# Sinkhorn attention with a max-of-two MoE layer: the zero matmuls, the GpSimd queue and the way W2 is turned

## The chip, the cores and the metric

The kernel runs on one core of one Trainium2 chip. The metric is the device time of one execution in microseconds (us), as the median of several executions. Engines are TensorE (PE; its weight loads are PEld), VectorE (DVE), ScalarE (ACT), GpSimd (POOL), SyncE (SP, which here only issues DMAs), and the 16 DMA engines.

## What is computed

Four batches, eight heads, 768 positions of 64 numbers. Each head's sequence is cut into 8 blocks of 96. Five Sinkhorn steps turn an 8x8 table per head into a soft permutation P, which mixes the blocks of k and v; each block of q attends to its mixed block. The heads are joined to 3072 tokens of 512 numbers, which go through a layer with two parallel weights and an elementwise maximum.

```python
for _ in range(5):
    P = np.exp(P - np.max(P, axis=-1, keepdims=True))
    P = P / (np.sum(P, axis=-1, keepdims=True) + 1e-09)
    P = P / (np.sum(P, axis=-2, keepdims=True) + 1e-09)
k_sorted = np.einsum('bhij,bhjcd->bhicd', P, k_b)
v_sorted = np.einsum('bhij,bhjcd->bhicd', P, v_b)
attn = softmax(scale * q_b @ k_sb.T)          # within each block
x = (attn @ v_sb)                             # -> 3072 x 512
out = np.maximum(x @ w1, x @ w2) @ w_out
```

## The kernel before

The order of instructions on each engine is that of the program text; nothing reorders it. Semaphore waits tie the engines together. Four PSUM buffers of 4 KB per partition serve all products in turn, so a product waits for the eviction of an earlier one. Inputs are loaded and cast to bf16 by DMAs on GpSimd's queue, in text order[...].

*Opening.* `keep_streaming` (L82) issues matmuls of zeros on TensorE: 86 of 142 columns at first, then six of 512 in each of Sinkhorn steps 4 and 5, each six waiting for a small memset on DVE (`late_zeros`). Meanwhile ACT and DVE make the Sinkhorn steps (L272 to L285), ending with p_bf. Between them DVE makes masks (`masks`), the batch 0 selections (`selections(0, nc.vector)`) and, later, two copies into maskJ (L824). GpSimd builds the identity `ident`, issues v0, k0 and q0 loads, then makes the selections of batches 1 to 3 and `one_j`, then issues all weight loads: W2 and W1 in columns, then W_out.

*Block diagonals and sorts.* `block_diagonals_first` (L367, L374) multiplies one_j and sel_v with p_bf, and DVE forms bd_k and bd_v. `sort_k` (three parts) and `sort_v` (four parts of 16 of the 64 columns) mix the blocks on TensorE; `turn_v` has laid v out by column first, on ACT and, for the last 16 of the 96 positions in a block, on DVE. Evictions go to ACT ("A") or DVE ("D") as the letter in the list says.

*Front.* The string `front` is the hand-written order of batch 0: k, v, tq (turn of q), SC (scores and exponential, eight units), VA (values, eight units), F (a request for zero matmuls in the next SC, VA or h unit), tx (turn of x), tw (turn of W2, two units of 16 transposes on TensorE), diff (W1 - W2), h (the hidden layer: two halves "a" and "b" per unit), pe (block diagonals of the other batches). Since max(h1, h2) = relu(h1 - h2) + h2, the kernel computes relu(x(W1 - W2)) W_out + x (W2 W_out). The first two quarters of W1 - W2 are made on GpSimd after the weight loads; the loads of k1, and later q1, v1, v2 and k2, follow them on GpSimd's queue.

*W2 W_out.* `w2_transposes` puts W2 with d_ff on the partitions into w2T, over PSUM; `w_product` (L668, four units) multiplies it with W_out.

*Passes.* Each batch then has numbered units on TensorE (the hidden layer, for batch 0 the four w_product in places 8 to 11, then twelve half output tiles), and a dictionary, `first_tail` for batch 0 and so on, says which steps of the next batch come after which unit: KS (key sorts), TQ, TURN (turn of v on DVE), SC, VS (value sorts), VA, TR (turn of x by DMA transpose on SP), pair_q (a copy of q on DVE), and `q_transposes` (DMA transposes on SP for batches 2 and 3).

Of the kernel before, what the change touches and what calls it, by code (L numbers as in the profile page):

```python
# [10 lines left out]
FP32 = mybir.dt.float32  # L11
# [5 lines left out]
def kernel(  # L17
# [16 lines left out]
    nc = tc.nc  # L34
# [34 lines left out]
    def ps_bf16(name):  # L69
        return psum.tile([128, 2048], BF16, tag="ps", name=name)  # L70
# [123 lines left out]
    load_k(0)  # L194
    load_q(0, True)

    sel_v, sel_k = {}, {}

    def selections(b, eng=nc.gpsimd):
# [12 lines left out]
            out=sel_k[b], in_=ident[0:G, b * 8 : b * 8 + 8].to_broadcast([G, 8, 16])  # L212
        )

    for b in range(1, B):
        selections(b)
    one_j = const.tile([G, 8 * 130], BF16, tag="one_j", name="one_j")
    nc.gpsimd.memset(one_j, 0.0)
    nc.gpsimd.tensor_copy(
        out=one_j.rearrange("g (j x) -> g j x", x=130)[:, :, 0:128].rearrange(  # L220
            "g j (h w) -> g j h w", w=16
        )[:, :, :, 0:2],
        in_=ident[0:G, 0:8].to_broadcast([G, 8, 2, NB]).transpose([0, 3, 1, 2]),
    )

    for t in range(2):
        load_w_columns(w2_sb, moe_w2, t, t + 1)
        load_w_columns(w1_sb, moe_w1, t, t + 1)
    load_w_columns(w2_sb, moe_w2, 2, 4)
    load_w_columns(w1_sb, moe_w1, 2, 4)  # L230
    load_w(wo_sb, moe_w_out)

    def w_difference(t, eng=None):
        n = DFF // 4
# [6 lines left out]
        if not eng:  # L241
            load["D"] += 600

    w_difference(0, nc.gpsimd)
    w_difference(1, nc.gpsimd)
    load_k(1)


    def turn_v(rows, eng, c0, c1):
# [39 lines left out]
            op=ALU.mult,  # L289
        )  # L290


    id64 = const.tile([128, 64], FP32, tag="id64", name="id64")
    maskJ = const.tile([128, 7, NB], FP32, tag="maskJ", name="maskJ")
    maskM = const.tile([128, 2, 8], FP32, tag="maskM", name="maskM")

    def masks(part):

# [161 lines left out]
    def sort_k(b, t, n=0, eng=None):  # L460
        kv = k_raw[b].rearrange("p (c d) -> p c d", d=D)
        ps = ps_f32("k_ps")
        keep_streaming(ps, n)

        for c in range(16):
            for par in range(2):
                m = (c + 8 * par) % 16
                r0 = par * 64
                nc.tensor.matmul(  # L469
                    ps[r0 : r0 + 64, m * 64 : (m + 1) * 64],  # L470
                    kv[r0 : r0 + 64, t * 16 + m, :],
                    bd_k[b][r0 : r0 + 64, :],
                    start=True,
                    stop=True,
                )
# [166 lines left out]
    w2T = big.tile([128, NFB, DMODEL], BF16, tag="w2T", name="w2T")  # L642
    wc = big.tile([128, HP, DMODEL], BF16, tag="wc", name="wc")

    def w2_transposes(t, eng):
        ps = ps_bf16("tw_ps")
        for n in range(16):
            fb, dmt = t * 4 + n // 4, n % 4
            nc.tensor.matmul(  # L649
                ps[:, n * 128 : (n + 1) * 128],  # L650
                w2_sb[:, dmt, fb * 128 : (fb + 1) * 128],
                ident,
                is_transpose=True,
                start=True,
                stop=True,
            )
        return lambda: evac(
            w2T[:, t * 4 : t * 4 + 4, :].rearrange("p f d -> p (f d)"),
            ps,
            2048,  # L660
            two_x=True,
            eng=eng,
        )

    def w_product(dmt):
# [119 lines left out]
    """.split()  # L785
    fills = [0]

    def fills_due():
# [3 lines left out]
    def front_step(step):  # L792

        eng = step[-1] if step[-1] in "AD" else None
        name = step[:-1] if eng else step
        kind = name.rstrip("0123456789ab")
        n = [int(x) for x in name if x.isdigit()]
        if kind == "F":
            fills[0] = 512
        elif kind == "k":  # L800
            sort_k(0, n[0], 1024 if step == front[0] else 0, eng)
        elif kind == "v":
            sort_v(0, n[0], 0, eng)
        elif kind == "tq":
            q_transposes(0, n[0], eng)
        elif kind == "SC":
            scores(0, n[0], fills_due())
        elif kind == "VA":
            values(0, n[0], fills_due())
        elif kind == "tx":  # L810
            x_transposes(0, n[0], eng)
        elif kind == "tw":
            w2_transposes(n[0], eng)()
        elif kind == "diff":
            w_difference(n[0])
        elif kind == "pe":
            block_diagonals([(0, 2), (0, 3), (1, 1), (1, 2), (1, 3)], 2)
        elif name[-1] == "a":
            moe_h_products(0, n[0], n[1], (0, 2), fills_due())
        else:  # L820
            moe_h(0, n[0], n[1], eng, (1, 3))

    for c, n, m in [(2, 2, 0), (4, 3, 1)]:
        nc.vector.tensor_copy(  # L824
            out=maskJ[:, c : c + n],
            in_=maskJ[:, m].to_broadcast([128, NB, n]).transpose([0, 2, 1]),
        )
    for step in front[:-26]:
        front_step(step)

    load_q(1)
# [14 lines left out]
    def sorts_and_scores(b):  # L846
# [27 lines left out]
    second_tail = {  # L874
        0: [lambda: q_transposes(2, 0), lambda: q_transposes(2, 1)],
        2: KS,
        4: SC[0:2],
        5: [VA[0]],
        6: SC[2:4],
        7: [VA[1], TR[0]],  # L880
        8: [VA[2], TURN[0]],
        9: [VA[3], TR[1], TURN[1]],
        10: SC[4:7],
        11: [VA[4], TURN[2]],
        12: [VA[5], TR[2], TURN[3], lambda: load_k(3), lambda: load_q(3)],
        13: [VA[6]],
        14: SC[7:8] + VS[0:2],
        15: [VA[7], TR[3]],
        16: VS[2:4],
        17: [lambda: pair_q(3, 0)],  # L890
        18: [lambda: pair_q(3, 1)],
    }
    SC, VA, TR, KS = sorts_and_scores(3)
# [69 lines left out]
```

## Time and profile before

| what | us |
|---|---|
| median of 9 executions | 167.37 (166.86 to 168.1) |
| the profiled execution | 168.1 |
| its span | 166.3 |
| TensorE busy | 160.5 |
| ACT, DVE, POOL busy | 83.1, 76.6, 32.2 |
| first exponential of batch 0 starts | 19.09 |
| first matmul of the hidden layer | 24.07 |
| GpSimd's first and second W1 - W2 start | 19.38, 22.17 |
| first w_product starts | 40.39 |
| first output product starts | 50.22 |

A line of the chain or the timeline gives start and duration in us, the engine, the line of the kernel or the tile, and how many instructions it merges. A line of the stage view gives, after the stretch, the busy time and the number of instructions of each engine. A line of the DMA view gives destination, source, the issuing queue, and the median time from issue to landing. SPq and POOLq are the issuing sides of SP and GpSimd. The page cuts the span into 40 slices of 4.16 us; a digit is a busy share in tenths. Matmuls are pipelined, so a mean duration of one (371 ns for 512 columns) is longer than the distance between two.

Loads through 62 us come in the order of GpSimd's queue: v0, k0, q0 (786 KB each in bf16), W1 and W2 (1.05 MB each), W_out (1.05 MB), k1, q1, v1 and v2, k2, q2, v3.

### The profile page before, as it was taken

How to read it: one execution, taken by the hardware profiler on the slowest of the kernel's cores; microseconds unless marked ns; L12 is line 12 of the kernel's file. 1: busy time of each engine (PE TensorE's matmuls, PEld its weight loads, DVE VectorE, ACT ScalarE, POOL GpSimd, SP SyncE). 2: the span in 40 equal slices, each digit the busy share in tenths (PEclk: the TensorE clock that was granted, in tenths of full speed). 3: DMA queues.
4: the chain of work that ended last, by engine and by line, in shares of the span. 5: the costliest groups of instructions: out<-in, count | busy, mean ns of one | idle time of the engine just before them, and what ended most of it. 6: DMA issues, size and time to landing. Idle time of an engine off the chain costs nothing.

```text
span 166.3 us, 4562 instructions
## 1 busy us (share of the span) xinstructions
PE 160.5 (96%) x2018; PEld 97.3 (58%) x2018; DVE 76.6 (46%) x173; ACT 83.1 (50%) x102; POOL 32.2 (19%) x55
## 2 busy tenths in 40 slices
PE   7999899999999999999899999999999999999992
PEld 7967778756554555557555544575655445654451
DVE  4859788556375564525258775070632420000011
ACT  3584994927239846055651344466456306652020
POOL 7997586150204000000004120000000000000000
PEclk9999999999999999999999999999999999999999
DMA  3999999999999996689602999989025284000333
GB/s 41 205 206 197 198 209 204 210 203 211 210 185 213 217 233 103 174 114 173 131 0 55 157 222 175 201 228 109 0 51 173 49 162 141 0 0 0 126 130 126
DMA packets 30404, 23.90 MB, mean 144 GB/s; under 512 B 16752, under 2 KB 25200, under 8 KB 30384
## 3 DMA queue, kind: packets, MB, share of 16 engines
q0 software_dynamic: 11040, 13.37, 48.2%
q1 hardware_dynamic: 19200, 10.17, 28.7%
q8 instruction: 16, 0.26, 0.6%
q10 hardware_dynamic: 144, 0.07, 0.1%
q14 instruction: 4, 0.03, 0.1%
HBM read 26.75 MB, written 6.29 MB: 199 GB/s over the span
## 4 chain that ended last, share of the span: by engine, by line
PE 85%; DVE 4%; DMA 4%; issue 2%; ACT 2%; ACTq 0%
PE out_ps L715 34%; PE h_ps L688 23%; PE fill_ps L82 7%; PE o_ps L586 4%; PE wc_ps L668 4%; DMA qT<-q_pair 4%; PE s_ps L559 4%; PE k_ps L469 2%; PE tq_ps L444 2%; ACT e L567 1%; DVE v_dc L257 1%; PE v_ps L534 1%; PE tw_ps L649 1%; PE v_ps L490 1%; PE tx_ps L624 1%
## 5 line engine op out<-in xcount | busy, mean ns | idle before, releaser
L715 PE MATMUL out_ps<-wo_sb,g 128*128 128x512 bf16 (+2 forms) x200 | 48.3, 371 | 0.1
L688 PE MATMUL h_ps<-xT,w_sb 128*128 128x384 bf16 x256 | 44.5, 326 | 0.0
L688 PEld LDWEIGHTS <-w_sb 128*128 128x128 bf16 x256 | 24.0, 98 | 15.6
L702 ACT ACTIVATE g<-h_ps 128x768 bf16<-128x768 f32 x27 | 21.8, 810 | 17.9 <-PE h_ps L688 17.8
L567 ACT ACTIVATE e<-s_ps 96x768 bf16<-96x768 f32 x32 | 23.8, 805 | 13.7 <-PE s_ps L559 13.5
L715 PEld LDWEIGHTS <-g 128*128 128x128 bf16 x200 | 17.1, 98 | 15.8
L715 PE MATMUL out_ps<-wc,xT 128*128 128x512 bf16 (+2 forms) x100 | 24.8, 370 | 0.0
L108 ACT COPY o<-out_ps 128x1024 f32<-128x1024 f32 x10 | 10.1, 1012 | 28.3 <-PE out_ps L715 25.6
L603 DVE TENSOR_TENSOR x<-o_ps,rs 96x512 bf16<-96x512 f32 x32 | 22.0, 687 | 1.1
L715 PEld LDWEIGHTS <-xT 128*128 128x128 bf16 x100 | 9.6, 97 | 11.2
L586 PEld LDWEIGHTS <-e 96*128 96x128 bf16 x256 | 11.8, 97 | 5.9 <-DVE v_sb L110 0.2
L597 DVE RECIPROCAL rs<-o_ps 96x8 f32<-96x8 f32 x32 | 6.4, 201 | 17.8 <-PE o_ps L586 17.7
L750 DVE COPY o<-out_ps 128x512 f32<-128x512 f32 (+1 forms) x2 | 1.2, 625 | 27.6 <-PE out_ps L715 27.6
L586 PE MATMUL o_ps<-v_sb,e 96*128 96x65 bf16 x256 | 12.9, 193 | 0.0
L108 ACT CAST v_sb<-v_ps 96x1024 bf16<-96x1024 f32 x10 | 9.8, 1015 | 2.5 <-PE v_ps L490 0.9
L110 DVE CAST kT<-k_ps 128x1024 bf16<-128x1024 f32 x7 | 8.3, 1215 | 5.8 <-PE k_ps L469 5.8
L704 DVE TENSOR_SCALAR g<-h_ps 128x768 bf16<-128x768 f32 x5 | 4.8, 956 | 12.3 <-PE h_ps L688 12.3
L559 PE MATMUL s_ps<-qT,kT 64*128 64x96 bf16 x256 | 8.6, 204 | 1.1 <-DMA qT<-q_pair 0.6
L559 PEld LDWEIGHTS <-kT 64*128 64x128 bf16 x256 | 6.1, 94 | 5.9 <-issue 3.1
L160 POOL DMA_DIRECT2D v_raw<-in_k_dram x3 | 2.4, 819 | 36.8 <-DVE rs L597 36.7
L82 PE MATMUL fill_ps<-fill 128*128 128x142 bf16 x86 | 8.3, 283 | 1.2 <-DVE fill L73 1.2
L110 DVE CAST v_sb<-v_ps 96x1024 bf16<-96x1024 f32 x6 | 7.3, 1216 | 4.5 <-PE v_ps L534 2.2
(96 smaller groups left out, 144.5 us busy)
## 6 DMA issues: line engine op xcount, KB each, us to landing
out_dram<-o SPq DMA_DIRECT2D x11, 512.0 KB, 3.3
v_raw<-in_v_dram POOLq DMA_DIRECT2D x8, 384.0 KB, 13.1
k_raw<-in_k_dram POOLq DMA_DIRECT2D x9, 256.0 KB, 10.0
w_sb<-in_moe_w_dram POOLq DMA_DIRECT2D x4, 256.0 KB, 8.3
w_sb<-in_moe_w_dram POOLq DMA_DIRECT2D x2, 512.0 KB, 11.0
wo_sb<-in_moe_w_out_dram POOLq DMA_DIRECT2D x2, 512.0 KB, 14.8
v_raw<-in_v_dram POOLq DMA_DIRECT2D x3, 256.0 KB, 4.9
q_raw<-in_q_dram POOLq DMA_DIRECT2D x4, 192.0 KB, 9.1
```

The costliest lines, as they stand in the source:

```text
L82: nc.tensor.matmul(ps[:, 0:w], w0, fill[:, 0:w], start=True, stop=True)
L108: nc.scalar.copy(out=out_ap, in_=in_ap)
L110: nc.vector.tensor_copy(out=out_ap, in_=in_ap)
L559: nc.tensor.matmul(ps[:, h2 * 512 + ii * 128 : h2 * 512 + ii * 128 + BLK], kT[b][rows, (hp * 8 + i) * BLK : (hp * 8 + i) * BLK + 128], rhs ...
L567: nc.scalar.activation(out=e[:, 0 : 8 * BLK].rearrange("p (t c r) -> p t c r", t=8, r=R), in_=ps[0:BLK] .rearrange("p (t f) -> p t f", t=8 ...
L586: nc.tensor.matmul(ps[:, h2 * 512 + ii * 65 : h2 * 512 + (ii + 1) * 65], e[:, (h2 * 4 + ii) * BLK : (h2 * 4 + ii) * BLK + 128], v_sb[:, m0 ...
L597: nc.vector.reciprocal(out=rs, in_=ov[:, :, :, 64])
L603: nc.vector.tensor_tensor(out=x, in0=ov[:, :, :, 0:D], in1=rs.to_broadcast([BLK, 2, 4, D]), op=ALU.mult,)
L668: nc.tensor.matmul(ps[:, 0:512], w2T[:, fb, dmt * 128 : (dmt + 1) * 128], wo_sb[:, fb, :], start=(fb == 0), stop=(fb == NFB - 1),)
L688: nc.tensor.matmul(h_ps[ch, t][:, m * 512 : m * 512 + TCH], w1_sb[:, hp, fb * 128 : (fb + 1) * 128], xT[:, b % 2, ch, hp % 2, hp // 2, :], ...
L702: nc.scalar.activation(out=g, in_=src, func=AF.Relu)
L715: nc.tensor.matmul(dst, g_tiles[b, ch, m // 2][:, m % 2, off : off + 128] if m < NFB else xT[:, b % 2, ch, hp % 2, hp // 2, off : off + 12 ...
```

## The change

- The first zero matmuls: 92 of 118 columns in place of 86 of 142. Those ahead of the first key sort: 640 columns in pieces of 320 in place of 1024 in pieces of 512. In `front` there is one more F, and two in a row now add up.
- GpSimd makes the selections of batch 0 and the two maskJ copies; DVE made them before. `one_j` is cleared as 32-bit words.
- GpSimd's queue is gated by three two-element copies into `seen`: the first reads p_bf, the second a piece of kT that the first key sort writes, the third the end of what the third transpose of W2 writes. The first W2 columns are issued after the first; the other weights after the second; the loads from q1 on after the third. Selections of batches 1 to 3 stand between the weight issues.
- W2 is turned by four DMA transposes on SP, one for each 128 columns of d_model, in place of 32 transposes on TensorE with two evictions. SP issues them ahead of every output store.
- `front` has a new order: the second key part first, scores of the second half of each sequence before the first half, later h units in another order.
- `first_tail` and `second_tail` have new places: key sorts and turns of q after w_product, value sorts at 17 to 19 in place of 12 to 14, values at 20 to 23 in place of 15 to 22, pair_q(2) in the second pass.

```diff
-    for b in range(1, B):
-        selections(b)
     one_j = const.tile([G, 8 * 130], BF16, tag="one_j", name="one_j")
-    nc.gpsimd.memset(one_j, 0.0)
+    nc.gpsimd.memset(one_j.bitcast(U32), 0)
...
+    selections(0)
-    for t in range(2):
-        load_w_columns(w2_sb, moe_w2, t, t + 1)
-        load_w_columns(w1_sb, moe_w1, t, t + 1)
-    load_w_columns(w2_sb, moe_w2, 2, 4)
-    load_w_columns(w1_sb, moe_w1, 2, 4)
-    load_w(wo_sb, moe_w_out)
...
-    w_difference(0, nc.gpsimd)
-    w_difference(1, nc.gpsimd)
-    load_k(1)
...
-        keep_streaming(ps, n)
+        keep_streaming(ps, n, most=320)
...
-    def w2_transposes(t, eng):
-        ps = ps_bf16("tw_ps")
-        for n in range(16):
-            fb, dmt = t * 4 + n // 4, n % 4
-            nc.tensor.matmul(
...
+    def w2_transposes(dmt):
+        nc.sync.dma_start_transpose(
+            out=w2T[:, :, dmt * 128 : (dmt + 1) * 128],
+            in_=w2_sb[:, dmt, :],
         )
...
-    keep_streaming(ps_f32("fill_ps"), 86 * 142, most=142)
+    keep_streaming(ps_f32("fill_ps"), 92 * 118, most=118)
...
-            selections(0, nc.vector)
...
+    for c, n, m in [(2, 2, 0), (4, 3, 1)]:
+        nc.gpsimd.tensor_copy(
+            out=maskJ[:, c : c + n],
+            in_=maskJ[:, m].to_broadcast([128, NB, n]).transpose([0, 2, 1]),
+        )
...
+    seen = const.tile([128, 3, 2], BF16, tag="seen", name="seen")
+    nc.gpsimd.tensor_copy(out=seen[0:G, 0], in_=p_bf[:, NB - 1, NB - 2 :])
+    load_w_columns(w2_sb, moe_w2, 0, 1)
+    selections(1)
+    selections(2)
...
     front = """
-        k0D k1A k2D v1D v2A v3A tq0D v0A tq1D SC1 SC0 F1
-        SC2 VA1 SC5 VA0 SC3 F2 VA2 SC4 F0 tx0D SC6 VA3
-        SC7 h00a VA4 tx1A tw0D h01a VA5 h01bA diff2 h00bA VA7 tx2A
-        tw1A h02a VA6 h02bA h11a diff3 tx3A h12a h03a h12bD h10a h10bA
-        pe2 h11bD h03bA h13a h13bA
+        k1A k0A v1D k2A v2A v0D tq0D v3A tq1D SC4 SC5 F2
+        F3 VA4 SC6 SC7 VA5 F0 SC0 VA6 SC1 VA7 F1 SC3
+        tx2D SC2 tx3D VA1 h10a VA0 VA2 h10bA h11a tx0A h11bA diff3
+        VA3 diff2 h13a h01a tx1D h03a h13bD h03bD h01bA h12a pe2 h00a
+        h02a h00bD h02bA h12bA
     """.split()
...
-            fills[0] = 512
+            fills[0] += 512
...
-            sort_k(0, n[0], 1024 if step == front[0] else 0, eng)
+            sort_k(0, n[0], 640 if step == front[0] else 0, eng)
...
-    for c, n, m in [(2, 2, 0), (4, 3, 1)]:
-        nc.vector.tensor_copy(
...
+    front_step(front[0])
+    c0 = int(front[0][1]) * 16
+    nc.gpsimd.tensor_copy(out=seen[:, 1], in_=kT[0][:, c0 : c0 + 2])
+    load_w_columns(w1_sb, moe_w1, 0, 1)
+    load_w_columns(w2_sb, moe_w2, 1, 2)
+    selections(3)
+    load_w_columns(w1_sb, moe_w1, 1, 2)
+    load_w_columns(w1_sb, moe_w1, 2, 4)
+    load_w_columns(w2_sb, moe_w2, 2, 4)
+    load_w(wo_sb, moe_w_out)
+    for dmt in range(HP):
+        w2_transposes(dmt)
+    w_difference(0, nc.gpsimd)
+    w_difference(1, nc.gpsimd)
+    load_k(1)
+    nc.gpsimd.tensor_copy(out=seen[:, 2], in_=w2T[:, NFB - 1, 382:384])
...
     first_tail = {
-        7: KS,
-        9: [TQ[0], TURN[0]],
-        10: [SC[0], TQ[1], TURN[1]],
-        11: SC[1:4] + TURN[2:4] + [lambda half=half: load_v(3, half=half) for half in range(2)],
-        12: VS[0:3],
-        13: VS[3:6],
-        14: VS[6:8] + [SC[4]],
-        15: [VA[0], lambda: pair_q(2, 0)],
-        16: [VA[1], lambda: pair_q(2, 1)],
-        17: SC[5:8] + [TR[0]],
-        18: [VA[2]],
-        19: [VA[3], TR[1]],
-        20: [VA[4]],
-        21: [VA[5], TR[2]],
-        22: [VA[6], VA[7], TR[3]],
+        11: KS,
+        12: [TQ[0]],
+        13: [SC[0], TQ[1]],
+        14: SC[1:4] + TURN[0:2],
+        15: SC[4:5] + TURN[2:4] + [lambda half=half: load_v(3, half=half) for half in range(2)],
+        16: SC[5:8],
+        17: VS[0:3],
+        18: VS[3:6],
+        19: VS[6:8],
+        20: [VA[0], VA[1]],
+        21: [VA[2], VA[3], TR[0], TR[1]],
+        22: [VA[4], VA[5], TR[2]],
+        23: [VA[6], VA[7], TR[3]],
     }
...
     second_tail = {
-        0: [lambda: q_transposes(2, 0), lambda: q_transposes(2, 1)],
+        0: [lambda: pair_q(2, 0), lambda: pair_q(2, 1)],
+        1: [lambda: q_transposes(2, 0), lambda: q_transposes(2, 1)],
         2: KS,
-        4: SC[0:2],
-        5: [VA[0]],
-        6: SC[2:4],
-        7: [VA[1], TR[0]],
-        8: [VA[2], TURN[0]],
-        9: [VA[3], TR[1], TURN[1]],
+        5: SC[0:2],
+        6: [VA[0], TURN[0]],
+        7: SC[2:4],
+        8: [VA[1], TR[0], TURN[1]],
+        9: [VA[2], TURN[2]],
         10: SC[4:7],
...
```

More of the change, by code (lines that the diff above doesn't have):

```diff
@@ L195 @@
     load_q(0, True)
+    id64 = const.tile([128, 64], FP32, tag="id64", name="id64")
+    maskJ = const.tile([128, 7, NB], FP32, tag="maskJ", name="maskJ")
+    maskM = const.tile([128, 2, 8], FP32, tag="maskM", name="maskM")
     sel_v, sel_k = {}, {}
@@ L290, in sinkhorn @@
         )
-    id64 = const.tile([128, 64], FP32, tag="id64", name="id64")
-    maskJ = const.tile([128, 7, NB], FP32, tag="maskJ", name="maskJ")
-    maskM = const.tile([128, 2, 8], FP32, tag="maskM", name="maskM")
     def masks(part):
@@ L643 @@
     wc = big.tile([128, HP, DMODEL], BF16, tag="wc", name="wc")
-    def w2_transposes(t, eng):
-        ps = ps_bf16("tw_ps")
-        for n in range(16):
-            fb, dmt = t * 4 + n // 4, n % 4
[L649 to L662, printed above, removed]
+    def w2_transposes(dmt):
+        nc.sync.dma_start_transpose(
+            out=w2T[:, :, dmt * 128 : (dmt + 1) * 128],
+            in_=w2_sb[:, dmt, :],
         )
@@ L811, in front_step @@
             x_transposes(0, n[0], eng)
-        elif kind == "tw":
-            w2_transposes(n[0], eng)()
         elif kind == "diff":
@@ L821, in front_step @@
             moe_h(0, n[0], n[1], eng, (1, 3))
-    for c, n, m in [(2, 2, 0), (4, 3, 1)]:
-        nc.vector.tensor_copy(
[L825 to L828, printed above, removed]
+    front_step(front[0])
[14 more added lines that the diff above has]
+    nc.gpsimd.tensor_copy(out=seen[:, 2], in_=w2T[:, NFB - 1, 382:384])
+    for step in front[1:-26]:
         front_step(step)
@@ L874 @@
     second_tail = {
-        0: [lambda: q_transposes(2, 0), lambda: q_transposes(2, 1)],
+        0: [lambda: pair_q(2, 0), lambda: pair_q(2, 1)],
+        1: [lambda: q_transposes(2, 0), lambda: q_transposes(2, 1)],
         2: KS,
-        4: SC[0:2],
-        5: [VA[0]],
-        6: SC[2:4],
-        7: [VA[1], TR[0]],
-        8: [VA[2], TURN[0]],
-        9: [VA[3], TR[1], TURN[1]],
+        5: SC[0:2],
[3 more added lines that the diff above has]
+        9: [VA[2], TURN[2]],
         10: SC[4:7],
-        11: [VA[4], TURN[2]],
-        12: [VA[5], TR[2], TURN[3], lambda: load_k(3), lambda: load_q(3)],
-        13: [VA[6]],
+        11: [VA[3], TR[1], TURN[3]],
+        12: [VA[4], lambda: load_k(3), lambda: load_q(3)],
+        13: [VA[5], TR[2]],
         14: SC[7:8] + VS[0:2],
-        15: [VA[7], TR[3]],
+        15: [VA[6]],
         16: VS[2:4],
-        17: [lambda: pair_q(3, 0)],
+        17: [VA[7], TR[3], lambda: pair_q(3, 0)],
         18: [lambda: pair_q(3, 1)],
```

## The prediction

> **What bounds the kernel now.** I read the engine shares of the page first, then the busy time by stage, then the chain of waits in order of time, and last the timeline of the stages that the change edits.
>
> ```profile
> PE 160.5 (96%) x2018; PEld 97.3 (58%) x2018; DVE 76.6 (46%) x173; ACT 83.1 (50%) x102; POOL 32.2 (19%) x55
> DMA  3999999999999996689602999989025284000333
> ```
>
> TensorE is busy for 160.5 of 166.3 us; nothing else passes half. But the DMA row is full in slices 2 to 15, up to about 62 us, so the first third has two limits: TensorE in program order, and loads that arrive just in time. The busy time by stage (TensorE, weight load, DVE, ACT, POOL, clock, DMA share, GB/s) gives the front:
>
> ```profile
> 12.04:18.70 6.66, 6.54 (x221) 5.53 (x221) 5.86 (x11) 4.00 (x5) 4.55 (x7) 1.00 1.39 201
> 18.70:24.14 5.44, 4.91 (x112) 3.51 (x109) 4.22 (x10) 5.24 (x8) 4.09 (x2) 1.00 1.31 202
> 24.14:38.83 14.69, 14.69 (x161) 10.08 (x163) 10.05 (x21) 8.80 (x11) 6.36 (x12) 1.00 1.23 208
> 38.83:52.32 13.49, 13.36 (x246) 7.66 (x247) 6.82 (x9) 7.36 (x11) 2.52 (x5) 1.00 1.13 200
> ```
>
> Sorts (DVE 5.86 of 6.66: evictions bound it), scores (ACT 5.24 of 5.44: exponentials bound it), then from 24.14 us on TensorE without a gap. The chain shows what stands in those stages:
>
> ```profile
> 1.20 10.90 PE fill_ps L82 x98
> 12.10 0.30 PE pe L367 x8
> ...
> 25.48 0.89 PE tw_ps L649 x16
> ...
> 29.19 0.89 PE tw_ps L649 x16
> ...
> 40.46 3.56 PE wc_ps L668 x16
> ```
>
> The zero matmuls at the start are themselves on the chain: the timeline has the last Sinkhorn step on DVE, which writes p_bf, from 11.06 to 11.27 us, yet the first matmul that reads it starts at 12.04. TensorE is 0.77 us late from filler. The two W2 turns cost 0.89 us each on a TensorE that is full.
>
> [...] the weight loads of L82, counted by the microsecond, double at about 7 us, though the page's clock column reads full throughout:
>
> ```profile
> 5.00:6.00 1.00, 1.00 (x9) 1.00 1.05 209
> 8.00:9.00 1.00, 1.00 (x18) 1.00 1.09 203
> ```
>
> [...] two qT transposes, 786 KB, were issued at 73.78 and had landed at 80.21[...], and beside loads they are slower still. [...]
>
> ```profile
> qT<-q_pair SPq DMA_TRANSPOSE x1, 6.4
> xT<-x SPq DMA_TRANSPOSE x1, 8.5
> ```
>
> The second was issued at 101.09 with q3 and an output store in flight (196 KB in 8.5 us to landing).
>
> **The change, part by part.**
>
> *Filler.* [...] So filler ends 0.57 us sooner, and the first product that reads p_bf starts at 11.47. p_bf itself comes at 11.19: the two sel_v copies that leave DVE stretched the fourth Sinkhorn step from 1.76 to 1.84 us. TensorE remains the later one: gain 0.57. On POOL the selections, one_j and mask copies end by about 9.8 (rows of 0.23 to 0.5 us after the last q issue at 7.97), well before use: nothing. The shorter fill ahead of the first key sort is hidden, since that sort waits for bd on DVE (12.70, then 12.91).
>
> *Sorts.* Now k1, k0, k2, v2, v3 leave by ACT at 1.01 us and v1, v0, tq0, tq1 by DVE at 1.2 and 0.96. Before, bd is ready at 12.70, the first k1 eviction starts on ACT at 14.15 (its products stood second, and ended at 14.05). After, bd is ready at 12.13, k1's 32 products (0.57) run first, and ACT starts at 12.97 and makes five evictions to 18.0. DVE ends the last turn of v at 13.3, evicts v1 from 14.15 to 15.37, v0 from 15.75 (its PSUM buffer is k0's, free at 15.0) to 16.97, tq0 to 17.93. The two mask copies (0.23) leave this row of DVE work. The first exponential starts near 18.45, not 19.09: 0.64, so the filler's gain and 0.07. The eight exponentials still pace the scores (5.97 us); one more fill of 512 columns stands under them and costs nothing. The last score ends at 23.50 instead of 24.14.
>
> *W2 turns.* 32 matmuls leave TensorE, 2 x 0.89 = 1.78 us, with evictions of 1.87 on ACT and 1.23 on DVE. After the last score the old order had 14.65 us of matmuls to 38.83; the new one has 8 x 1.30 of h, 4 x 0.24 of values, 3 x 0.34 of tx, 0.25 of pe (all durations from the chain): 12.65, so the front ends at 36.15. Two things could stop it there. GpSimd now issues the weights after p_bf and after the first key eviction (about 14.0), each 0.76: last wo issue near 20.4, differences at 2.12 each done by 22.5 and 24.6; h10 and h11 want them at 24.0 and 25.8. That fits. The DVE difference waits for the last W2 columns: 3.93 + 0.52 MB at 205 GB/s lie before their end at 25.3, plus 2 us to the semaphore (so the first difference, 17.5 by bytes, began at 19.38): 27.3 + 0.68 against a need at 27.65. I charge 0.3: front end 36.45, 2.4 earlier.
>
> *The transposes.* SP has nothing else queued then; the four need all of W2, so issue starts at 27.3. They move 1.05 MB beside 0.57 MB of W_out and 0.79 MB of k1 still due. With turns taken evenly at a total of 195 GB/s, three are through when 1.57 MB have moved, 8 us after 28.3, landed at 37.4; the fourth at 40. w_product reads one transpose each at 36.45, 38.3, 40.1 and 41.9. All four fit, with 2 us or less to spare.
>
> *The gate.* POOL's third seen copy holds q1, v1, v2, k2, q2 and v3 behind the third transpose. q1 is issued at 37.6 to 38.5 and lands by 44.5; its turn is wanted at 46.7 (w_product 7.3, keys 1.64, one output part 1.35). v1 and v2 land at 48.5 and 52.3; the value sorts want them, turned, at 57.5. k1 lands at 42.2 for 43.8. So later loads are hidden too.
>
> *The later order.* Scores spread over three units give back 0.4 of the 0.65 us that TensorE lost around 50 to 52.3 (exponentials on the chain). But the value sorts now stand just ahead of values: five evictions on ACT behind three exponentials, and v_sb complete about 0.3 us late. The x transposes of batch 1 are issued only at units 21 to 23 in place of 17 to 22: the second is issued some 1.9 us after its values (two reciprocals of 0.20, two products of 0.69) and lands 3.8 later, while TensorE reaches its readers in about 4.3 us: 1.1 lost. Against this the qT wait at 79 to 81 (0.6 + 0.1) goes, as scores start at unit 5, not 4. Together +0.3.
>
> Sum: -2.4 + 0.3 = **-2.1 us**. The profiled execution took 168.1 (span 166.3 and 1.8 around it), which would give 166.0; it was the slowest of nine. From the median, 167.37, I forecast **165.3**.
>
> **Unknown costs, from both sides.** Transposes of this shape: at best their plain bytes (5.2 us at 205 GB/s, no loss), at worst 8.5 us each as the row above: fourth landed after 60. I take even turns. POOL's timing beside DVE: nothing, or 1 us on the differences. The x wait: 0 to 2 us. [...]
>
> **Rivals.**
>
> A. *More is kept.* The x wait does not arise (landing 2.8 us, as some xT rows have) and the second pass loses less of its 0.82 us of TensorE idle (71.5 to 105.6, by stage): -2.4 - 0.3 - 0.7 = -3.4, 163.9. For it: the chain runs over DVE and DMA, not TensorE, at 73.8 to 80.2 and 91 to 97.7, so there is something to win. Against: ACT and DVE get less time between value sorts and values.
>
> B. *Gained in front, given back behind.* TensorE leads, and the same loads, later by the transposes' bytes, end the wait at the first turn of v or of q1: 1.05 MB at 195 GB/s is 5.4 us of transfer put into a row that is full to 62 us, of which 3 to 5 us of slack are eaten. A loss of 2 cancels: 167.4. For it: the DMA row. Against: q2 and v3 are now wanted a whole pass later.
>
> C. *Slower.* One mechanism: beside the loads the transposes get less than an even share, and w_product, in TensorE's order, waits with everything behind it. It decides when the fourth lands after 41.9, and the kernel gets slower once it lands after 44.0 (or the third after 42, by q1). At 4.8 us each, between the qT row alone and the worst xT row, the fourth lands at 28.3 + 19.2 = 47.5: 5.6 lost - 2.1 = +3.5, at 4.0 each +0.3; between them, at 4.4 each, +1.9: I put this case at 169.3. For it: the 8.5 row. Against: only 1.36 MB of loads compete, and they run dry by about 40.
>
> **How the numbers follow.** Forecast 0.46 (-1.0 to -2.9), A 0.18, B 0.12, C 0.24. Less than 0.5 us (0.3%) is what a measurement of this kernel can hardly tell from none; B lies mostly there (0.08), with 0.02 each way. Faster 0.46 + 0.18 + 0.02 = 0.66, same 0.08, slower 0.24 + 0.02 = 0.26. The range runs from 163.2 (A with its best costs) to 169.2, leaving the worse half of C out; the forecast's own is 164.5 to 166.4.
>
> **What would show it.** The one_j products near 11.5; first exponential near 18.5; last h_ps row of the front ending near 36.5 with no tw_ps; four DMA_TRANSPOSE rows on SP from about 27, landing by 40; no idle of L643 on w2T; q1's issue near 38; PE idle of about 1 us at the start of the second pass. I am wrong if TensorE stops ahead of wc_ps or tq_ps, if a chain through w2T appears, or if the front ends after 37.5.

## The result, and the profile after

The changed kernel takes 172.51 us (median of 10 runs, 170.65 to 173.57), the kernel before 167.4: a ratio of 1.027 with an interval from 1.024 to 1.030. It is slower by 4.5 us by the ratio and 5.1 by the medians, where 165.3 was forecast. The profiled execution took 170.92, with a span of 168.8 for 166.3. Of its twelve executions, with the profiled one, five took 170.7 to 171.7 at a granted clock of 0.998 or above, and seven 172.5 to 173.6 at 0.99; the profile shows one of the five.

The page's engine shares and its DMA row of the kernel after:

```profile
PE 158.3 (94%) x1993; PEld 93.5 (55%) x1993; DVE 75.6 (45%) x169; ACT 80.4 (48%) x100; POOL 33.5 (20%) x62
DMA  3999999997999999999704999984025253000333
```

TensorE has lost 2.2 us of work, and yet the span is 2.5 us longer: waits of 4.7 us are new. The DMA row, full up to slice 15 before (62 us), is now full up to slice 19 (80 us). The same four stages as shown of before (length; busy time of TensorE, weight load, DVE, ACT, POOL; clock, DMA share, GB/s):

```profile
12.04:18.70 6.66, 6.49 (x227) 5.49 (x220) 5.15 (x7) 5.61 (x7) 6.37 (x15) 1.00 1.39 198
18.70:24.14 5.44, 5.02 (x109) 3.62 (x109) 4.25 (x11) 5.30 (x8) 4.88 (x4) 1.00 1.28 186
24.14:38.83 14.69, 13.02 (x113) 7.96 (x112) 9.85 (x22) 4.73 (x7) 1.91 (x4) 1.00 1.23 200
38.83:52.32 13.49, 13.49 (x199) 7.32 (x198) 2.99 (x3) 5.07 (x7) 5.70 (x10) 1.00 1.01 179
```

The third row had TensorE busy throughout; now 1.67 us are idle in it. What ended those waits stands in the list of waits of the kernel after (who waited for what: us in total, times, longest):

```profile
POOL seen L821 <- DMA w2T<-w_sb: 13.8, 1, 13.8
PE h_ps L663 <- DMA xT<-x: 2.7, 1, 2.7
PE wc_ps L643 <- DMA w2T<-w_sb: 1.0, 1, 1.0
PE h_ps L663 <- DVE w_sb L231: 0.7, 1, 0.7
```

The chain of the kernel after puts them in order of time (start, length, what):

```profile
17.40 10.18 DMA w_sb<-in_moe_w_dram
...
27.67 10.37 DMA w2T<-w_sb
...
38.09 7.08 PE wc_ps L643 x32
...
53.96 1.50 ACT e L556 x2
55.45 0.90 ACT o L108
56.36 0.72 ACT e L556
...
64.46 1.22 DVE v_sb L110
...
69.76 5.25 DMA xT<-x
```

The opening is faster than forecast: the one_j product starts at 11.14 (12.04 before) and the first exponential at 18.13 (19.09). Up to w_product the gain holds in part. Behind it the chain leaves TensorE three times: for exponentials with an output eviction among them on ACT at 54 to 57 us, for v_sb at 64.5, and for a transfer of x at the start of the second pass. The first of these is no new loss: the chain before has exponentials at 50 to 52 us too, and TensorE is busy for 9.89 of the 10 us from 50 to 60, before 9.87. For v_sb TensorE waits 0.5 us, for x 2.7. That pass starts 3.06 us later than before (74.43 for 71.37), the third 2.33 later (107.76 for 105.43): 0.7 comes back in the second pass, and nothing after it.

### The profile page after: what moved, and what is told of

Read it like the earlier page. It is cut to its first block, busy times and chain, and to the rows that moved or that the text cites. A ratio compares the mean times of both kernels' runs of the same rounds, so it can differ in the third digit from the quotient of the medians.

```text
span 168.8 us, 4520 instructions
## 1 busy us (share of the span) xinstructions
PE 158.3 (94%) x1993; PEld 93.5 (55%) x1993; DVE 75.6 (45%) x169; ACT 80.4 (48%) x100; POOL 33.5 (20%) x62
## 4 chain that ended last, share of the span: by engine, by line
PE 69%; DMA 16%; DVE 5%; ACT 3%; POOL 2%; issue 1%; SPq 0%; ACTq 0%
PE out_ps L690 35%; PE h_ps L663 19%; DMA w2T<-w_sb 6%; DMA w_sb<-in_moe_w_dram 6%; PE wc_ps L643 4%; PE k_ps L458 3%; PE o_ps L575 3%; DMA xT<-x 3%; PE s_ps L548 3%; POOL w_sb L189 2%; ACT e L556 1%; PE v_ps L523 1%; PE tq_ps L433 1%; DMA p_sb<-in_sort_net_dram 1%; DVE colsum L276 1%
## 5 line engine op out<-in xcount | busy, mean ns | idle before, releaser
L108 ACT COPY o<-out_ps 128x1024 f32<-128x1024 f32 x9 | 9.1, 1013 | 28.3 <-PE out_ps L690 25.6
L575 PEld LDWEIGHTS <-e 96*128 96x128 bf16 x256 | 10.9, 98 | 6.4 <-DVE v_sb L110 1.0
L110 DVE CAST kT<-k_ps 128x1024 bf16<-128x1024 f32 x5 | 5.9, 1221 | 17.6 <-PE k_ps L458 17.6
L725 DVE COPY o<-out_ps 128x512 f32<-128x512 f32 (+1 forms) x2 | 1.2, 625 | 27.6 <-PE out_ps L690 27.6
L575 PE MATMUL o_ps<-v_sb,e 96*128 96x65 bf16 x256 | 12.3, 193 | 0.7 <-DVE v_sb L110 0.5
L110 DVE CAST v_sb<-v_ps 96x1024 bf16<-96x1024 f32 x7 | 8.5, 1219 | 5.6 <-PE v_ps L523 2.7
L108 ACT CAST v_sb<-v_ps 96x1024 bf16<-96x1024 f32 x9 | 8.9, 1007 | 2.2 <-PE v_ps L500 0.9
L643 PE MATMUL wc_ps<-wo_sb,w2T 128*128 128x512 bf16 x32 | 7.1, 379 | 1.0 <-DMA w2T<-w_sb 1.0
## 6 DMA issues: line engine op xcount, KB each, us to landing
wo_sb<-in_moe_w_out_dram POOLq DMA_DIRECT2D x2, 512.0 KB, 13.3
```

The costliest lines, as they stand in the source:

```text
L108: nc.scalar.copy(out=out_ap, in_=in_ap)
L110: nc.vector.tensor_copy(out=out_ap, in_=in_ap)
L575: nc.tensor.matmul(ps[:, h2 * 512 + ii * 65 : h2 * 512 + (ii + 1) * 65], e[:, (h2 * 4 + ii) * BLK : (h2 * 4 + ii) * BLK + 128], v_sb[:, m0 ...
L643: nc.tensor.matmul(ps[:, 0:512], w2T[:, fb, dmt * 128 : (dmt + 1) * 128], wo_sb[:, fb, :], start=(fb == 0), stop=(fb == NFB - 1),)
```

## The experiments

Four theories were open. **P**: the DMA engines take turns between SP's ring and GpSimd's by packets, not by bytes; transposes, in small packets, starve beside loads. **T**: the new order of the tails costs time by itself. **K**: the long waits let the granted clock fall, which makes the seven executions at 0.99. **R**, the rival of P: transposes of this kind are simply slow.

### Packets

The DMA view of the kernel after, by stretches of 2 us (packets, MB, share of 16 engines; q0 is GpSimd's ring, q1 is SP's), at 32 to 34 and then at 38 to 40:

```profile
q0 software_dynamic: 201, 0.36, 94.8%
q1 hardware_dynamic: 199, 0.05, 18.3%
...
q1 hardware_dynamic: 2113, 0.52, 124.2%
```

201 packets against 199, but 0.36 MB against 0.05. Alone, the transposes move ten times as much, 0.52 MB in 2 us or 260 GB/s. That already speaks against R. To see it without the gate and the new orders, the kernel before got nothing but the four DMA transposes in place of the two W2 turns:

```diff
-        SC7 h00a VA4 tx1A tw0D h01a VA5 h01bA diff2 h00bA VA7 tx2A
-        tw1A h02a VA6 h02bA h11a diff3 tx3A h12a h03a h12bD h10a h10bA
+        SC7 h00a VA4 tx1A h01a VA5 h01bA diff2 h00bA VA7 tx2A
+        h02a VA6 h02bA h11a diff3 tx3A h12a h03a h12bD h10a h10bA
...
+    for dmt in range(HP):
+        w2_transposes(dmt)
```

> The kernel before with the four DMA transposes of W2 alone, issued on SP as soon as W2 has landed, without a gate on GpSimd's queue, and without the two units on TensorE. Loads then run beside them until about 57 us. Theory P (packets in turn): some 4096 packets of 256 B against loads at 50 to 200 packets per us: the last transpose lands near 50 us or later, w_product (ready at 39) waits 8 us or more, with lost clock beside: 173 to 182. Rival R (10 us by themselves, whatever runs beside): they land by 40, nothing waits, 165.5 to 166.5.

Measured: 188.93 us (184.83 to 190.52). The loads, now without a gate, run beside the transposes to the end. The DMA view at 44 to 46 and at 52 to 54 us, then two of the waits of this kernel:

```profile
q0 software_dynamic: 64, 0.32, 86.2%
q1 hardware_dynamic: 63, 0.02, 7.0%
...
q0 software_dynamic: 129, 0.27, 99.9%
q1 hardware_dynamic: 131, 0.03, 17.5%
```
```profile
POOL w_sb L143 <- DMA w2T<-w_sb: 20.6, 1, 20.6
PE wc_ps L654 <- DMA w2T<-w_sb: 13.3, 2, 7.1
```

Packet for packet the rings are even, to within two; by bytes SP gets a ninth to a sixteenth of what GpSimd gets. How much depends on the loads' packets. At 39 to 41 us theirs are small, under 800 bytes (0.29 MB in 373), and SP gets a third:

```profile
q0 software_dynamic: 373, 0.29, 90.9%
q1 hardware_dynamic: 374, 0.10, 36.2%
```

P holds, and R falls. The size is larger than expected, and the clock has a part in it: its mean was 0.95 in all four executions, while TensorE waited 13.3 us for w2T. The gate in the changed kernel, which looked like a cost, is what keeps this from happening there.

### k1 behind the transposes

In the changed kernel k1 is the only later load ahead of the gate. Here it goes behind it.

```diff
-    load_k(1)
     nc.gpsimd.tensor_copy(out=seen[:, 2], in_=w2T[:, NFB - 1, 382:384])
+    load_k(1)
```

> The load of k1 is issued behind the third transpose of W2 in place of ahead of it, so that from about 31 us the transposes have the DMA engines to themselves. Theory P (each DMA engine takes packets in turn from the two rings, and a transpose packet of 256 B stands against a load packet of 1 to 2 KB): the first transpose lands near 34 us in place of 38.1, w_product no longer waits (it starts at 37.0), and the time falls by 1.0 to 1.5 us. Rival R (a transpose of this shape takes some 10 us by itself): it lands at 37 to 38 again, w_product waits as before, and the time stays at 172.5 or grows, as k1 comes later.

Measured: 171.05 (170.35 to 174.47), ratio 1.020 (1.015 to 1.026). SP's timeline has the four transposes issued in 7.8 us, not 11.4, and the third has landed at 35.8, not 39.9; w_product no longer waits for w2T. Its waits:

```profile
PE h_ps L663 <- DMA xT<-x: 2.9, 1, 2.9
PE tq_ps L433 <- DMA q_raw<-in_q_dram: 0.6, 1, 0.6
```

The first transpose took 6.3 us to landing, not 10.4, so the loads beside them decide how long they take, as P has it. But q1, now behind k1, comes late for its turn, and the x wait remains: the front's wait was the smaller part. The two runs at full clock, 170.35 and 170.39, are only some 0.4 us below those of the kernel after (170.65 to 171.67, median 170.81), so most of the 1.5 us between the medians (172.51 and 171.05) is the clock.

### The x wait

v3 is the load in GpSimd's ring when x is to be transposed. SP's timeline of the kernel after has three transposes issued over 5.71 us from 67.98, the first landed 6.3 us later; its DMA view at 68 to 70 us, and an issue of SP in the view at 64 to 66:

```profile
q0 software_dynamic: 66, 0.32, 77.3%
q1 hardware_dynamic: 68, 0.14, 19.9%
...
out_dram<-o SPq DMA_DIRECT2D x1, 512.0 KB, 8.9
```

SP's 68 packets carry 2 KB each (0.14 MB), where those of the W2 transposes carry 256 bytes (0.05 MB in 199). They belong to the output store that SP issued ahead of the transposes. The store takes turns with v3 and needs 8.9 us to landing, for a median of 3.3, and in the trace the packets of 256 bytes start only at about 71 us, when the store is nearly through. So v3 holds the x transposes up mostly through the store ahead of them.

A run held v3 behind the second x transpose, and another did that together with k1 behind the gate.

```diff
-        15: SC[4:5] + TURN[2:4] + [lambda half=half: load_v(3, half=half) for half in range(2)],
+        15: SC[4:5] + TURN[2:4],
...
-        21: [VA[2], VA[3], TR[0], TR[1]],
+        21: [VA[2], VA[3], TR[0], TR[1], after_x]
+        + [lambda half=half: load_v(3, half=half) for half in range(2)],
```

> The four loads of v3 are issued behind the second x transpose of batch 1 (a two-element copy that reads it) in place of some 15 us sooner. Theory P: the first x transpose lands near 71.5 in place of 74.4, TensorE's wait of 2.7 us at the start of the second pass falls below 0.8, and, as no long gap is left there, the runs at clock 0.99 become rare: 168.3 to 169.5 in all. Rival R: the x transposes take 5 to 6 us from issue as before, the wait stays, and the time is 172 to 173.

> Both moves of loads. Theory P: the two gains add, 167.2 to 168.3, no wait over 0.8 us on w2T or xT. Rival R: no less than 172.

Both missed: 184.19 (177.68 to 185.97) and 184.15 (179.42 to 186.1). The first x wait did go (0.5 us), but v3 now stands beside the fourth x transpose and those of qT. The chain of the run with v3 alone, its DMA view at 88 to 90 us, and its stretches ahead of and from 86 us:

```profile
74.09 20.47 DMA xT<-x
```
```profile
q0 software_dynamic: 71, 0.35, 97.8%
q1 hardware_dynamic: 69, 0.02, 8.4%
```
```profile
78.00:86.00 8.00, 2.29 (x46) 1.45 (x41) 1.95 (x2) 1.82 (x2) 0.00 (x0) 0.81 1.25 49
86.00:94.00 8.00, 0.00 (x0) 0.00 (x0) 0.00 (x0) 0.00 (x0) 0.00 (x0) 0.50 1.10 174
```

Where the x transpose issued ahead of it, with GpSimd's ring empty, landed in 2.9 us, the fourth took 20.5. The time was missed since I asked only which transposes v3 would leave, and not which it would meet. Turns by packets fit the second half of these 20.5 us, at 174 GB/s in all. In the first half both rings together moved only 49 GB/s; taking turns doesn't explain that, and its cause is open. The clock, at 0.50 from 83 us on, adds to the loss.

### The clock

Zero matmuls stand in the two waits, 11 of 512 columns ahead of the second pass and 4 ahead of w_product.

```diff
         ps = ps_f32("wc_ps")
+        keep_streaming(ps, 4 * 512 if dmt == 0 else 0)
...
-        units = [lambda ch=ch, t=t: moe_h(b, ch, t) for ch in range(2) for t in range(4)]
+        units = [
+            lambda ch=ch, t=t: moe_h(b, ch, t, n=11 * 512 if (b, ch, t) == (1, 0, 0) else 0)
+            for ch in range(2)
+            for t in range(4)
+        ]
```

> The changed kernel with 11 zero matmuls of 512 columns (2.4 us) ahead of the first hidden unit of the second pass and 4 (0.9 us) ahead of the first w_product, where TensorE waits 2.7 and 1.4 us for transposes. Theory K (the runs at mean clock 0.99 lose about 1.7 us because a gap on TensorE drops its clock to half for a few us): the gaps are filled, all runs are at clock 1.0, and the median is 170.5 to 171.2 in place of 172.5. Rival: the split of the changed kernel's runs into 170.7 and 172.6 has another cause; then the split stays and the median is 172 to 173.

Measured: 171.7 (171.04 to 172.01), ratio 1.025 (1.021 to 1.029). The time is a little above what was expected. In the profile, of the slowest of the four, the zeros are no longer than the waits that they replace (2.4 us for 2.7, 0.9 for 1.0), but the opening is 0.3 later, the wait for the W2 columns 0.4 longer, and TensorE waits 0.8 for q1. Still, all four runs had a clock of 1.00; none fell to 0.99, though four are few.

All runs together say more. In three kernels TensorE waits 2.7 to 2.9 us at one place (the kernel after, k1 behind the transposes, and v3 behind the qT transposes, below), and 12 of their 20 executions have a mean clock of 0.99 or less. In four kernels with the same opening and no such wait (this one and, below, W2 on TensorE, the old first tail, both old tails) none of 40 has. So K holds as far as this: such a wait makes a fall likely. It is not the only cause, since 3 of 19 executions of the kernel before, beside the last run below, have a clock of 0.99 or less too, and its longest wait behind the start is 0.6.

In the profiles the clock falls to half (0.50 in the row from 86 us above): for 17.1 us in the run with v3 behind x, and for 3.4 in that with v3 behind the qT transposes (a mean of 0.59 from 94 to 98 us). One fall of 3.4 us at half clock loses 1.7 us, about what lies between the two groups of the kernel after (medians of 172.7 and 170.8). Ahead of the fall TensorE was idle for 2.8 us in the latter, and in the last run below for no more than 0.5 at once behind the start. The falls of the kernel after itself are in no profile.

### W2 on TensorE again

The changed kernel with the two W2 turns back in its front (tw0A ahead of diff3, tw1A ahead of h01b), and without the gate:

```diff
+        elif kind == "tw":
+            w2_transposes(n[0], eng)()
...
-    for dmt in range(HP):
-        w2_transposes(dmt)
...
-    nc.gpsimd.tensor_copy(out=seen[:, 2], in_=w2T[:, NFB - 1, 382:384])
```

> The changed kernel with W2 turned on TensorE again (two units in its new front order, evicted by ACT) and without the gate on w2T, so that the loads from q1 on are issued some 15 us sooner. Theory P: no wait for w2T; the front ends 1 us later than in the changed kernel by 1.8 us of matmuls less its waits; v3 has landed before the x transposes, so the wait at the second pass is under 1.2 us, and the clock stays at 1.0: 167.3 to 169. Rival R2 (the new places in the tails cost the time by themselves, whatever the loads do): 170 to 172.

Measured: 169.25 (168.4 to 169.69), ratio 1.012 (1.009 to 1.016), just above what was expected. So W2 by DMA with its gate costs 3.3 us. But the median of the kernel after falls among its executions at lower clock. At full clock its five have a median of 170.81, and these four of 169.25: 1.6 us are waits and transfers, 1.7 the clock. Where the waits lie is seen at the start of the second pass, 72.09 for 74.43. This kernel's x wait, and the DMA view of it at 70 to 72 us:

```profile
PE h_ps L677 <- DMA xT<-x: 0.5, 1, 0.5
```
```profile
q1 hardware_dynamic: 991, 0.25, 66.1%
```

GpSimd's ring is empty there. The timelines of GpSimd (start, length) show why. Of the kernel after, and then of this one:

```profile
41.01 2.10 POOL L169 DMA_DIRECT2D v_raw<-in_v_dram  x4
...
57.85 1.56 POOL L169 DMA_DIRECT2D v_raw<-in_v_dram  x3 [3.09 <-DVE v_dc L250]
```
```profile
56.22 1.55 POOL L169 DMA_DIRECT2D v_raw<-in_v_dram  x3 [0.92 <-DVE v_dc L250]
```

With the gate, the last v loads are issued 1.6 us later into rings that still hold what the gate kept back, and end at about 72 us; without it they end by 68, and the store ahead of x takes 4.3 us to landing, not 8.9. First out_ps comes at 46.74 with the transposes and at 47.25 without: in front the change of W2 wins 0.5 us, as TensorE work less its waits, and at the second pass it is 2.3 behind. Of the 2.8 lost between, 2.7 are the x wait, through a load that nobody waited for; the kernel here has 0.5 of that wait still to come, behind its first two matmuls of the pass.

### The tails

On top of that, the first tail of the kernel before (without its two q pairings, which the new second tail does), and then both its tails:

```diff
     first_tail = {
-        11: KS,
-        12: [TQ[0]],
...
+        7: KS,
+        9: [TQ[0], TURN[0]],
...
```

> Base: e5_w2_on_pe (169.25 us). The first tail is that of the kernel before, the second that of the kernel after (pair_q at its unit 0). Theory F (the whole 1.7 us between e5 and e7_old_tails lie in the first tail: x transposes at its end, the split exponentials, v_sb): 167.0 to 167.8, x wait below 0.5. Rival S (part of it lies in the second tail): 168.2 to 169.2, with TensorE idle between 71 and 105 us above that of e7_old_tails.

> As the one before, and with the two tails of the kernel before: only the opening, the sorts, the front order, GpSimd's gates on p_bf and kT and the zero matmuls are those of the change. Theory P: the start of the scores 0.96 us sooner is kept to the end: 166.0 to 166.9. Rival R3 (the opening's gain is lost again in the front or at the loads): 167.2 to 168.5.

Measured: 167.22 (166.88 to 167.85), ratio 0.9995 (0.998 to 1.001), and 167.59 (167.36 to 168.43), ratio 1.0016 (1.000 to 1.003). The first hit, the second missed by 0.7 in favour of its rival. So the new first tail costs 2.0 us, and the new second tail wins some 0.4, with intervals that still overlap. (The kernel before took 167.38 beside the run with both old tails, and 167.35 beside the other.) The engines' busy time by stretches, with the new first tail (W2 on TensorE) and then with the old one:

```profile
60.00:71.00 11.00, 10.35 (x173) 5.92 (x167) 8.63 (x14) 4.84 (x5) 0.00 (x0) 1.00 0.80 200
71.00:75.00 4.00, 3.49 (x34) 2.10 (x33) 3.61 (x9) 1.75 (x2) 0.00 (x0) 1.00 0.66 143
```
```profile
60.00:71.00 11.00, 11.00 (x121) 6.05 (x120) 5.24 (x12) 3.22 (x4) 0.00 (x0) 1.00 0.87 175
71.00:75.00 4.00, 4.00 (x26) 2.32 (x24) 1.84 (x5) 2.45 (x3) 0.00 (x0) 1.00 0.86 78
```

Crowded into units 17 to 23, value sorts and values leave DVE 12.24 us of work in 15 (8.63 and 3.61); spread from unit 12 on it was 7.08 (5.24 and 1.84), and TensorE never stopped. TensorE's own idle time can't be read from the first of these traces: it holds 2006 of 2025 matmuls, and a missing one leaves a hole of up to 0.16 us. Of the 0.65 us that look idle from 60 to 71, such holes make more than half. The kernel after, whose trace is complete, waits 0.5 there for v_sb. That the crowding causes the 2.0 us fits these rows and the x wait of 0.5 us, which is gone with the old tail, but no run tests it alone; the two spans differ by 1.2 (166.6 and 165.4), and the rest is in no profile.

What of the opening's 0.9 us is left with the old tails? Nothing: w_product starts at 40.38, before at 40.39. The chain of the kernel with both old tails, and two waits of its TensorE:

```profile
17.49 10.45 DMA w_sb<-in_moe_w_dram
...
28.03 0.70 DVE w_sb L231
28.78 1.47 PE h_ps L677 x8
```
```profile
PE o_ps L575 <- ACT e L556: 0.4, 1, 0.4
PE h_ps L677 <- ACT w2T L108: 0.4, 1, 0.4
```

The new front wants the W2 columns as soon as the loads bring them: they are on the chain, and TensorE waited 0.3 for them in the run with the old first tail and 0.7 in the kernel after. Here the lead goes mostly to other things: 0.4 to the eviction of a W2 turn, whose place in this front I had chosen, 0.2 to one more fill of 512 columns, and some to waits in the scores, 0.4 and 0.2 where they were 0.3 and 0.2.

A last attempt at the x wait held v3 behind the qT transposes of batch 2, still with W2 on TensorE and the new tails, the turns of v3 two units later:

```diff
         1: [lambda: q_transposes(2, 0), lambda: q_transposes(2, 1), after_q]
+        + [lambda half=half: load_v(3, half=half) for half in range(2)],
```

> Base: e5_w2_on_pe (169.25 us; x wait of 2.8 us before the second pass). The two loads of v3 are held on GpSimd behind the last qT transpose of batch 2, and its four turns come two units later. Theory X (the 2.8 us wait for xT is there because the v3 loads stand beside the x transposes, and packets of the two rings alternate): the wait falls below 1.0 and the first h_ps of the second pass starts at 70.3 to 71.4 for 72.1; no transpose needs more than 8 us; time 167.0 to 168.3. Rival L (the x transposes are late because the order issues them late): the wait stays above 2 and the time at 168.9 to 169.8. If v3 then comes late for its turns, a wait on v_raw shows between 80 and 95 and takes the gain back.

Measured: 172.65 (171.15 to 173.3), ratio 1.031 (1.027 to 1.035). The base was misread: the 2.8 us that I named as its wait were the transfer's length on the chain, and TensorE waited 0.5, here too. So this run says nothing on X; it shows another price. v3 landed at 92.4, its turn stood on DVE waiting 3.4 us, the values' products queued behind it, and TensorE stopped for 2.8. The stretches after that:

```profile
90.00:94.00 4.00, 1.27 (x20) 0.56 (x18) 1.58 (x4) 1.50 (x2) 0.50 (x1) 0.98 1.13 176
94.00:98.00 4.00, 3.90 (x25) 1.80 (x26) 1.40 (x3) 0.81 (x1) 1.95 (x3) 0.59 0.75 111
```

After the stop TensorE is busy but at a mean clock of 0.59: part of the wait is paid a second time, as K has it.

### The opening alone

```diff
-    keep_streaming(ps_f32("fill_ps"), 86 * 142, most=142)
+    keep_streaming(ps_f32("fill_ps"), 92 * 118, most=118)
```

> The kernel before with 92 x 118 zero columns in place of 86 x 142, and nothing else. Theory: the zeros are on the chain; the first product that reads p_bf starts 0.5 to 0.6 us sooner and the time is 166.8 to 167.1. Rival: the gain is taken up by the evictions of the sorts or by the loads: 167.3 to 167.6.

Measured: 166.98 (166.58 to 170.22), ratio 0.9972 (0.9957 to 0.9987), as expected. The first product that reads p_bf starts at 11.31 for 12.04, the first exponential at 18.33 for 19.09, and 0.74 of it is still there at w_product (39.65 for 40.39). Half of it reaches the end.

With the new order of sorts on top, selections(0) on GpSimd too:

```diff
-        k0D k1A k2D v1D v2A v3A tq0D v0A tq1D SC1 SC0 F1
+        k1A k0A v1D k2A v2A v0D tq0D v3A tq1D SC1 SC0 F1
...
-            sort_k(0, n[0], 1024 if step == front[0] else 0, eng)
+            sort_k(0, n[0], 640 if step == front[0] else 0, eng)
```

> The kernel before with the 92 zero matmuls of 118, the order of sorts of the kernel after, all selections on GpSimd and the shorter fill ahead of the first key sort; scores and the rest of the front stay. Theory O (the order of sorts keeps what the filler gives, and scores, W2 turns and loads have slack of 0.3 us or more): first exponential at 18.1 to 18.3, time 166.5 to 167.0, as e6_before_fill (166.98) or up to 0.4 less. Rival W (the weights, issued after the selections, come later for the first h): 167.2 to 168.

Measured: 167.38 (167.07 to 170.56), ratio 0.9996 (0.997 to 1.002). The first exponential came at 18.21, as expected, and the time missed. In its profile TensorE stops for 0.78 us within the first product of values, with no releaser shown, and the first h starts at 24.09, not 23.39. A hole of 0.5 in the same place stands in the profile of the next kernel, whose front is that of the fill alone; so the order isn't shown to be its cause, and what is stays open.

Last, the two parts that had won: the fill, and the new second tail, in the kernel before.

```diff
-    keep_streaming(ps_f32("fill_ps"), 86 * 142, most=142)
+    keep_streaming(ps_f32("fill_ps"), 92 * 118, most=118)
...
-        0: [lambda: q_transposes(2, 0), lambda: q_transposes(2, 1)],
+        0: [lambda: pair_q(2, 0), lambda: pair_q(2, 1)],
+        1: [lambda: q_transposes(2, 0), lambda: q_transposes(2, 1)],
...
```

> The kernel before with the two parts that the runs so far show as gains: the 92 zero matmuls of 118 (e6_before_fill: 166.98) and the second tail of the kernel after (e11_old_first_tail less e7_old_tails: -0.37). Theory add (the second tail's gain is its own: the qT wait of 0.6 and TensorE's idle time between 75 and 105 us, 0.8 in the kernel before, go): 166.4 to 166.8, no qT wait of TensorE. Rival (the -0.37 was scatter, or hangs on the front of the kernel after): 166.9 to 167.4.

Measured: 166.61 (166.2 to 168.23) with 166.97 for the kernel before on the same chip, ratio 0.9974 (0.996 to 0.9987). TensorE is busy for all of 75 to 105 us. No qT wait shows, but the profile of the fill alone, with the old second tail, has none either. The ratio is that of the fill alone, so by the times the second tail's 0.4 isn't shown to add to it. The traces do show a gain in the second pass. From its first matmul of the hidden layer to that of the third pass it lasts 33.01 us here and 33.03 with the old first tail, against 33.43 with the fill alone and 33.60 with both old tails.

The profile is that of the slowest of the 16 executions (168.23), and shows why: the clock falls in the front, and the first h starts at 25.0.

```profile
22.00:23.00 1.00, 1.00 (x19) 0.86 (x17) 0.97 (x3) 0.74 (x2) 0.86 (x1) 0.55 1.24 206
23.00:24.00 1.00, 1.00 (x12) 0.37 (x9) 0.61 (x2) 0.30 (x1) 1.00 (x1) 0.50 1.26 216
```

Behind the start, TensorE had not waited longer than the 0.5 us of that hole.

## Why the prediction was wrong

**Filler: right, undersized.** The step gave 0.57 (first product at 11.47), an estimate of mine that no trace of before shows; it measured 0.9 in the changed kernel, and 0.7 with the fill alone. The first zeros, 8.31 us before, took 6.7 in the changed kernel and 6.2 with the fill alone. Counted by the microsecond, their weight loads double at about 7 us before, but at about 5 in the kernel after (12 from 4 to 5 us, 21 from 5 to 6). "TensorE remains the later one" did not hold. The first product now waits 0.2 us for p_bf on DVE, so a shorter fill would win nothing more.

**Sorts: right.** First exponential 18.45 forecast, 18.13 measured; from the first product on, 6.98 and 6.99.

**W2 turns: nearly right.** The front's last h ended at 37.1 for 36.45. The term "I charge 0.3" for the DVE difference was 0.7. I had the W2 columns landing at 27.3 and they landed at 27.6, which is no great miss; but the new front has nothing else to do there. The matmuls behind the last score, put at 12.65, took 13.1 without that wait.

**Transposes: the step that failed in kind is "with turns taken evenly at a total of 195 GB/s".** The even turns were my assumption, shown by no trace of before, and I counted them in bytes. By packets the split at 32 to 34 us was 199 to 201, by bytes 0.05 to 0.36 MB. The first transpose landed at 38.05 and the third at 39.85 for 37.4, and w_product, forecast without a wait, waited 1.0. The W2 transposes came to 260 GB/s alone (38 to 40 us in the kernel after) and to 10 to 50 beside loads (0.02 to 0.10 MB in 2 us). Rival C named this mechanism and put the point of decision at a fourth landing after 41.9. It landed at about 41.0, so C's price wasn't paid there.

**The gate: "so later loads are hidden too" failed, and costs most.** I followed q1, k1, v1 and v2 to their readers, and rightly: TensorE waits for none of them. v3 I let go, since it is wanted a pass later. But a load needs no reader to do harm: it held GpSimd's ring until 72 us, slowed the output store on SP's ring (8.9 us to landing for 4.3 without the gate), and the x transposes stood behind that store. The x wait, put at 1.1, was 2.7; with W2 on TensorE and no gate it was 0.5. The clock, some 1.7 of the medians' difference, was contained in no case.

**The later order: the term "together +0.3" was mis-sized.** The first tail costs 2.0. Of its named parts, exponentials -0.4 rested on 0.65 us that TensorE was said to lose around 50 to 52.3. That was read off the chain; the stage row has TensorE busy for 13.36 of 13.49 us there, so there was little to win, and nothing was won or lost (9.87 and 9.89 busy of the 10 us from 50). v_sb, +0.3, measured 0.5. The qT wait is gone, as forecast, but in the fill alone it is gone too. What fills the rest of the 2.0 is not shown.

Summed from the medians: fill -0.4, the rest of the front with W2 still on TensorE +0.6, second tail -0.4, first tail +2.0, W2 by DMA with its gate +3.3 (1.7 of it the clock), in all +5.1, which is 172.5 less 167.4. The sum closes by itself, as each part is one kernel less the one ahead of it. The forecast had -2.4 for the front and +0.3 behind it. Rival B, given back behind by late loads, was nearer in kind than C, but with the readers of q1 and v as its place, and so too small.

## What to carry to other kernels

Where two DMA rings are busy, count packets, not bytes: here a transpose in packets of 256 bytes moved a third of the loads' bytes where their packets were under 800 bytes, and a ninth to a sixteenth where they were larger. So keep every large load off the stretch in which a transpose is awaited, also one whose own reader is far away, and look at what stands ahead of the transpose on its own ring. Where a transfer is moved to a later time, list what it then meets, not only what it leaves. And a lead in front is worth what the next load lets through: with the fill alone, of 0.7 us at the first product, 0.4 reached the end.

## What the runs showed of the hardware

The even split by packets was finer than expected: 64 to 63, 129 to 131, 71 to 69. An x transpose took 2.8 us to landing alone (at 70 to 72 us, with W2 on TensorE), 6.3 behind a store that took turns with the end of v3, and 20.5 beside all of v3. After a TensorE wait of 2.8 us its clock fell to half for 3.4 us (v3 behind the qT transposes), and in the last run it fell where no wait behind the start had been longer than 0.5. In three kernels with a wait of 2.7 to 2.9 us, 12 of 20 executions have a mean clock of 0.99 or less, in four without one none of 40.
